# Small products of a scan split into two halves of heads, two GpSimd products taken a group earlier, and one integer step moved behind a mask, in a fused Mamba-2 scan and ELU feed-forward kernel

## The chip, the cores and the metric

The kernel runs on one core of one Trainium2 chip. The metric is the device time of one launch in microseconds (us). Before the change the median of three runs is 347.31 us (346.28 to 347.36). A profile is one more execution, recorded instruction by instruction.

The engines are named as in the profile: PE is the matrix engine TensorE, PEld its loading of weights, DVE is VectorE, ACT is ScalarE, POOL is GpSimd, and SP is the queue that issues nearly all transfers. L654 is line 654 of the kernel before the change.

## The reference: what is computed

A Mamba-2 scan in chunks, and then a feed-forward block with an ELU between its two products:

```python
# x (4, 8, 768, 32), a (4, 8, 768), B and C (4, 8, 768, 16); chunks of tokens per (batch, head)
cum = np.cumsum(log(a) of the chunk)
M = (C B^T) * exp(cum_i - cum_j) * causal
y = M x + (C state) * exp(cum)                     # inside the chunk + from the state before it
state = exp(sum of log a) * state + sum_j exp(cum_last - cum_j) B_j x_j^T
...
h = y_rows @ w_in            # (3072, 256) @ (256, 2048)
out = where(h > 0, h, exp(min(h, 0)) - 1) @ w_out   # @ (2048, 256)
```

All inputs are fp32. The result of the scan, with its heads side by side, is the input of the feed-forward block.

## The kernel before, in words

**Tiles of the scan.** A block `n` holds 256 tokens of one batch and all 8 heads; there are 12 blocks, and the scan works with chunks of 64 tokens, so a block has four, numbered by (u, v). Blocks 4 to 11 are handled in pairs (m, m+1). A pair needs, in this order: the decays L (a transfer from `flat`, a subtraction by `decay_sums`, L531 on POOL, an Exp on ACT, a mask on POOL); C scaled by exp(cum) (`turn_exp`, L459, here on POOL; its result is `cts`, the second half of the tile `bct`); `scores` (L577 on PE); `weigh` (L586 on DVE, gives M); `sums` (L607 on PE) and `states` (L622 and L624 on DVE, then a copy `Sx` masked by heads, L629 on POOL); `across` (L654 on PE: the part of y that comes from the state before a chunk); and `inside` (L672 on PE: M x, added to the same accumulators), after which y is shifted back to its place in `yT` (L689 on ACT, L687 on DVE).

**Small products.** `across` uses 32 rows by 64 columns of the array, at the position given by q (four pairs of heads, 32 rows each) and v. Its results go into four PSUM tiles y[t][v]: t is the half of the heads (q 0 and 1, or q 2 and 3). `inside` is called for one t at a time and has 64 rows by 32 columns. An fp32 product is two passes on PE, so that the profile counts two instructions for each product.

**Feed-forward.** For blocks 4 on, every fp32 product is put together from three products of shorter words. `l1_words` (L826) makes 128 columns of h for a pair of blocks: six passes of 128x512, into the PSUM tiles ps_w and ps_h. ACT reads ps_w into e (L834), DVE joins e and ps_h (L842), ACT takes Relu and Exp (L854, L855), DVE finishes the ELU (L861). A job then makes words of g for the second product: L916 on ACT, L917 on DVE (`g_low`), L893 on POOL (`g_words`). `second` is a generator: each step of it (here called a unit) is one slice of the second product, six passes of L975.

**Order.** Everything is written out by hand. For a pair of blocks n the loop over k = 0 to 15 issues one `l1_words`, `stage_scan(n, k)` for the scan of the next pair m, and some units of the second product for the pair before. At k = 9 come `scores`, at k = 10 `sums`, at k = 13 `across` and `inside`. This loop runs four times; the last has no scan left, so that `across` at k = 13 happens three times, for m = 6, 8 and 10. Pairs before that are handled elsewhere in the code (the pair (4, 5) calls `across` and `inside` without units between).

**PSUM.** There are eight banks. Seven are in the pool `p_a`, shared by all PE results, and one in `p_o`. A tile that takes a bank waits for the last reader of the tile that had it.

**Beginning.** The weights come as 64-bit floats. `w_sign` (L229), `w_high_a` (L237) and `w_high_b` (L244, a shift to the left) on DVE and `w_sum` (L254) on POOL make fp32 out of their words, piece by piece. `mask_heads(1)` (L476 on DVE) masks C of block 1 by heads for its `scores`.

The lines that the change touches are these:

```python
    def across(*ns, pool=p_a, tag="a"):
        y = [psum([P, len(ns), 2, Q], "ps_y") for _ in range(3)]
        y.append(pool.tile([P, len(ns), 2, Q], F32, tag=tag, name="ps_y"))
...
            if k == 13:
                y = across(m, m + 1, pool=p_o, tag="o")
                l2s(2)
                inside(y, m, m + 1, t=0)
                l2s(1)
                inside(y, m, m + 1, t=1)
```

Of the kernel before, what the change touches and what calls it, by code (L numbers as in the profile page):

```python
# [10 lines left out]
F32 = mybir.dt.float32  # L11
# [6 lines left out]
P = 128  # L18
# [15 lines left out]
def kernel(  # L34
# [56 lines left out]
    def psum(shape, name):  # L91
        return p_a.tile(shape, F32, tag="a", name=name)
# [129 lines left out]
    def w_sign(i, cols=slice(None), eng=nc.vector):  # L222
        w_parts_of(i)
        if eng is nc.gpsimd:
            eng.tensor_scalar(
                out=w_sgn[i][:, :, cols], in0=w_words(i)[1][:, :, cols].bitcast(mybir.dt.int32),
                scalar1=0.0, scalar2=2.0 ** 31, op0=ALU.is_lt, op1=ALU.mult)
            return
        nc.vector.tensor_scalar(  # L229
            out=w_sgn[i][:, :, cols], in0=w_words(i)[1][:, :, cols], scalar1=0x80000000,  # L230
            scalar2=None, op0=ALU.bitwise_and)
# [16 lines left out]
    def w_high(i):  # L248
        w_high_a(i)
        w_high_b(i)  # L250
# [222 lines left out]
    def mask_heads(n, eng=nc.vector):  # L473
        s = st[n]
        s["ctm"] = att.tile([P, 2, 2, P], F32, tag="ctm", name="ctm")
        eng.tensor_tensor(  # L476
            out=s["ctm"], in0=s["ct"].unsqueeze(2).to_broadcast([P, 2, 2, P]),
            in1=hmask2.unsqueeze(1).unsqueeze(3).to_broadcast([P, 2, 2, P]), op=ALU.mult)
# [158 lines left out]

        return 2 * D * v if n else 0

    def across(*ns, pool=p_a, tag="a"):  # L640


        y = [psum([P, len(ns), 2, Q], "ps_y") for _ in range(3)]
        y.append(pool.tile([P, len(ns), 2, Q], F32, tag=tag, name="ps_y"))
        y = [y[0:2], y[2:4]]
        for u in (1, 0):
            for at, n in enumerate(ns):
                for v in range(2):
                    Sx = starts.pop((n, u, v), None)
                    if Sx is None:  # L650
                        continue
                    for q in range(4):
                        rows, col = slice(32 * q, 32 * q + 32), (64 * q + shift(n, v)) % P
                        nc.tensor.matmul(  # L654
                            out=y[q // 2][v][col:col + 64, at, u],
                            lhsT=Sx[rows].rearrange("p k d -> p (k d)"),
                            rhs=st[n]["cts"][rows, u, Q * v:Q * v + Q],
                            start=(u == 1 and at == 0), stop=False,
                            tile_position=(32 * q, col), skip_group_check=True)
        return y  # L660

    def inside(y, *ns, t=None):

        for t in range(2) if t is None else (t,):
            for at, n in enumerate(ns):
                s = st[n]
                for u in range(2):
                    for v in range(2):
                        toks = slice(Q * v, Q * v + Q)
                        for q in range(4):  # L670
                            h, col = 4 * t + q, (D * q + shift(n, v)) % P
                            nc.tensor.matmul(  # L672
                                out=y[t][v][col:col + D, at, u],
                                lhsT=s["x"][toks, u, D * h:D * (h + 1)],
                                rhs=s["M"][h // 2][toks, u, h % 2], start=False, stop=True,
                                tile_position=(Q * v, col), skip_group_check=True)
            n = ns[0]
            if n // 2 not in yT:
                yT[n // 2] = ffn.tile([P, KC, 2, 2, P], F32, tag="yT", name="yT")
            out = yT[n // 2][:, t, n % 2:n % 2 + len(ns)]  # L680
            for v in range(2):
                k = shift(n, v)
                for at in (0, k) if k else (0,):
                    count, src = P - k, (at + k) % P
                    to, src = out[at:at + count, :, :, Q * v:Q * v + Q], y[t][v][src:src + count]
                    if t and (n == 1 or n > 4):
                        nc.vector.tensor_copy(to, src)  # L687
                    else:
                        nc.scalar.copy(out=to, in_=src)  # L689
        if t:  # L690
            for n in ns:
                st.pop(n)
# [414 lines left out]
    w_abs(3)  # L1107
    w_low(3, nc.scalar)
    w_sign(3)
    w_high(3)  # L1110
    mask_heads(1)
    turn_b(1)
    nc.scalar.activation(F[:, 1], F[:, 0], ACT.Exp)
    write_flat_exp()
# [209 lines left out]
    def stage_scan(n, k):  # L1324

        m = n + 2
        if k < 2:
            spread_exp(m + k)
        if k == 2:
            load_x(m)  # L1330
            load_x(m + 1)
        if 0 < k < 5 and (n > 4 or k > 1):
            turn_part(m + (k > 2), (k - 1) % 2)
        if k < 3:
            decay_exps(m + (k > 0), (k + 1) % 2)
        if k in (0, 1, 3, 4):
            decay_mask(m + (k > 1), (k + (k > 1)) % 2)
        if k in (5, 7):
            turn_part(m + k // 7, 2)
        if k in (6, 8):  # L1340
            scaled(m + k // 8, nc.gpsimd)
        if k == 10:
            turn_part(m, 3)
            turn_part(m + 1, 3)
        if k in (3, 5) and n > 4:
            load_b(m + (k > 3))
        if k in (6, 7) and m + 2 < NP:
            load_bc(m + k - 4)
        if k == 15 and m + 2 < NP:
            decay_exps(m + 2, 0)  # L1350

    for n in range(4, NP, 2):
        m = n + 2 if n + 2 < NP else None
        steps = second(n - 2)

        def l2s(count):
            for _ in range(count):
                next(steps)

        if n == 4:  # L1360
            l2s(1)
        if not m:
            scan_pools.close()
            late_pool = ctx.enter_context(tc.tile_pool(name="late", bufs=1))
        for k in range(16):
            if k < 13 and (n > 4 or k > 4):
                to_begin.append(lambda q=k + 3: job(n - 2, q))
            elif m and k > 12:
                to_begin.append(lambda q=k - 13: job(n, q))
            if not m and k in (4, 6, 8, 10, 12, 14, 15):  # L1370
                to_begin.append(lambda q=(4, 6, 8, 10, 12, 14, 15).index(k): late_job(q, late_pool))
            if k == 0 and n > 4:
                load_words(2)
            l1_words(
                n, k, m, [lambda q=q: weigh_two(m, q) for q in (2, 3) if m and k == 10],
                [lambda: states(m + 1)] if m and k == 11 else [])
            if k != 14 or not m:
                third_of_jobs()
            if n == 4 and k < 2:
                words_of_w(k + 2)  # L1380
            if n == 4 and 1 < k < 7:
                words_of_out(k + 1)
            if k in (2, 4, 6, 8, 10) and (k > 2 or n > 4):
                load_words(k // 2 + 2)
            if m and k == 14:
                nc.sync.dma_start(out=held, in_=yT[m // 2][Q:Q + 1, 0, 0, 0, Q:Q + 16])
            if m and k > 13:
                load_words(k - 14)
            if m:
                stage_scan(n, k)  # L1390
            begin_end()
            if n == 4 and k in (1, 2):
                low_of_w(k + 1)
                keep_words(k + 1)
            if n == 4 and 2 < k < 8:
                low_of_out(k)
            if not m:
                l2s(2)
                continue
            if k == 9:  # L1400
                l2s(1)
                scores(m, m + 1, pool=p_o, tag="o")
            l2s((2 - (n == 4 and k < 1), 2, 2, 2, 2, 2, 2, 2, 2, 1, 2, 2, 1, 0, 1, 0)[k])
            if k == 9:
                for q in range(2):
                    weigh_two(m, q)
            if k == 10:
                if m + 2 < NP:
                    for to in (m + 2, m + 3):
                        spread_cum(to)  # L1410
                sums(m, m + 1, pool=p_o, tag="o")
                states(m)
            if k == 13:
                y = across(m, m + 1, pool=p_o, tag="o")
                l2s(2)
                inside(y, m, m + 1, t=0)
                l2s(1)
                inside(y, m, m + 1, t=1)
            if k in (12, 13) and m + 2 < NP:
                decay_sums(m + k - 10)  # L1420
        if m:
            l2s(3)
        end_words()
        for _ in steps:
            pass
# [46 lines left out]
```

## Time and profile before

| | |
|---|---|
| runs | 346.28, 347.31, 347.36 us; median 347.31 |
| profiled execution | 345.99 us, of which the span of the profile is 344.1 us |
| granted clock of PE | 0.999 over the span |
| busy time in the span | PE 334.0, PEld 290.6, DVE 286.7, ACT 260.1, POOL 216.2 us |
| chain that ended last | PE 86%, DVE 5%, ACT 3%, POOL 2%, DMA 1%, issue 1% |
| `across` at k = 13, first start of L654 | 156.42, 208.06 and 260.55 us |
| the loop's first L826 of each pair that follows | 168.06, 220.50 and 272.4 us (about 52 us apart) |

The span runs from the first to the last instruction; the profiled execution is 1.9 us longer than its span. The chain that ended last is followed back from the end: at each step to what released the waiting instruction, or to the one before it on its engine. In a timeline row stand the start in us, the length in us from the first start to the last end of what is merged, the engine, the line, the operation, the tiles, the shape, the count of merged instructions, and in brackets the idle time of the engine before it with what ended it. Matmuls are pipelined: one pass of 128x256 lasts 0.28 us, but the next starts 0.12 us after it.

### The profile page before, as it was taken

Reading aid. Unit: us, or ns where it says so; the run is one execution under the profiler, and the core shown is the slowest. Engines: PE = TensorE matmul, PEld = TensorE weight load, DVE = VectorE, ACT = ScalarE, POOL = GpSimd, SP = SyncE. Lnnn points to the kernel's source line nnn. Section 1 sums busy time; section 2 is a strip of 40 time slices with the busy share of each in tenths; the row PEclk is TensorE's granted clock in tenths of the full one; section 3 lists DMA queues with packets and bytes.
Section 4 is the critical chain, followed back from the end, with each engine's and each line's share of the span. In section 5 each row is a group of like instructions: output and inputs, shape, how many; then the busy total and the mean of one; then the engine's idle time right before and its main releaser. Section 6 shows DMA issues by size and latency. Waiting matters only on the chain.

```text
span 344.1 us, 9650 instructions
## 1 busy us (share of the span) xinstructions
PE 334.0 (97%) x3742; PEld 290.6 (84%) x3742; DVE 286.7 (83%) x507; ACT 260.1 (76%) x537; POOL 216.2 (63%) x242
## 2 busy tenths in 40 slices
PE   8889999999999999999999998999998999999996
PEld 6568878888887888887899986898887899999995
DVE  2898998889797889896989987989995977997951
ACT  3887989699858699865898865798866688897601
POOL 5554545557989396989388968478965255775100
PEclk9999999999999999999999999999999999999999
DMA  8988979362578378660779390869340743240101
GB/s 145 244 221 192 316 132 257 71 153 76 187 143 314 128 208 273 201 175 10 270 193 231 105 284 20 272 192 187 105 168 2 277 137 146 79 161 0 33 0 61
DMA packets 82955, 54.79 MB, mean 159 GB/s; under 512 B 59038, under 2 KB 68574, under 8 KB 82910
## 3 DMA queue, kind: packets, MB, share of 16 engines
q1 hardware_dynamic: 80734, 53.98, 55.8%
q8 instruction: 29, 0.48, 0.6%
q10 hardware_dynamic: 2176, 0.20, 0.5%
q14 instruction: 16, 0.13, 0.1%
HBM read 44.53 MB, written 9.63 MB: 157 GB/s over the span
## 4 chain that ended last, share of the span: by engine, by line
PE 86%; DVE 5%; ACT 3%; POOL 2%; DMA 1%; issue 1%; DVEq 0%; POOLq 0%
PE ps_o L975 21%; PE ps_h L826 16%; PE ps_o L879 12%; PE ps_h L711 11%; PE ps_w L826 9%; PE ps_both L975 6%; PE ps_y L672 3%; PE ps_g L577 2%; PE ps_y L654 2%; DMA L<-flat 1%; DVE M L586 1%; PE ps_high L975 1%; DVE ps_h L842 1%; DVE g_low L917 1%; POOL bct L459 1%
## 5 line engine op out<-in xcount | busy, mean ns | idle before, releaser
L893 POOL TENSOR_TENSOR g_words<-g_words,g_low 128x512 fp32r<-128x512 f32 x62 | 82.4, 1332 | 55.6 <-DVE g_low L917 28.5
L975 PE MATMUL ps_o<-o_words,g_words 128*128 128x256 f32 x448 | 84.1, 285 | 0.0
L975 PEld LDWEIGHTS ps_o<-o_words,g_words 128*128 128x128 f32 x448 | 72.7, 190 | 6.2 <-POOL g_words L893 0.9
L854 ACT ACTIVATE e<-ps_h 128x512 f32<-128x512 f32 x72 | 43.1, 598 | 36.0 <-DVE ps_h L842 36.0
L861 DVE SCALAR_TENSOR_TENSOR g<-e,ps_h 128x512 f32<-128x512 f32 x72 | 49.3, 684 | 17.8 <-ACT e L855 15.8
L917 DVE SCALAR_TENSOR_TENSOR g_low<-g_words,g 128x512 fp32r<-128x512 f32 x72 | 63.4, 886 | 0.0
L975 PE MATMUL ps_o<-o_low,g_low 128*128 128x256 f32 x224 | 63.3, 283 | 0.0
L842 DVE SCALAR_TENSOR_TENSOR ps_h<-ps_h,e 128x512 f32<-128x512 f32 x72 | 49.8, 692 | 2.8 <-ACT e L834 2.8
L826 PE MATMUL ps_w<-y_both,w_words 128*128 128x512 f32 x144 | 48.7, 419 | 0.2 <-PE ps_h L826 0.2
L855 ACT ACTIVATE e<-e 128x512 f32<-128x512 f32 x72 | 45.5, 632 | 2.3
L834 ACT ACTIVATE e<-ps_w 128x512 f32<-128x512 f32 x72 | 42.0, 583 | 6.8 <-PE ps_w L826 6.8
L711 PE MATMUL ps_h<-yT,w_in 128*128 128x256 f32 (+1 forms) x208 | 45.1, 367 | 2.0 <-POOL w_in L254 1.1
L879 PE MATMUL ps_o<-w_out,g 128*128 128x256 f32 x192 | 45.5, 380 | 0.0
L826 PE MATMUL ps_h<-y,w_words 128*128 128x512 f32 x144 | 45.3, 395 | 0.0
L826 PE MATMUL ps_h<-y,w 128*128 128x512 f32 x144 | 44.7, 391 | 0.0
L916 ACT ACTIVATE g_words<-g 128x512 fp32r<-128x512 f32 x72 | 43.6, 624 | 0.0
L711 PEld LDWEIGHTS ps_h<-yT,w_in 128*128 128x128 f32 x208 | 36.4, 190 | 7.6 <-POOL w_in L254 1.6
L975 PEld LDWEIGHTS ps_o<-o_low,g_low 128*128 128x128 f32 x224 | 42.7, 191 | 0.0
L879 PEld LDWEIGHTS ps_o<-w_out,g 128*128 128x128 f32 x192 | 36.1, 190 | 5.5
L826 PEld LDWEIGHTS ps_h<-y,w 128*128 128x128 f32 x144 | 27.0, 188 | 6.3
L826 PEld LDWEIGHTS ps_h<-y,w_words 128*128 128x128 f32 x144 | 26.7, 188 | 6.6 <-PE ps_w L826 0.4
L826 PEld LDWEIGHTS ps_w<-y_both,w_words 128*128 128x128 f32 x144 | 23.5, 191 | 2.3 <-ACT e L854 0.6
(133 smaller groups left out, 555.7 us busy)
## 6 DMA issues: line engine op xcount, KB each, us to landing
w_words<-w_kept SPq DMA_DIRECT2D x28, 512.0 KB
w<-w_kept SPq DMA_DIRECT2D x28, 256.0 KB
L<-flat SPq DMA_DIRECT2D x20, 256.0 KB
w<-in_moe_w_out_dram SPq DMA_DIRECT2D x8, 512.0 KB
w_kept<-w_words SPq DMA_DIRECT2D x8, 512.0 KB
w<-in_moe_w_in_dram SPq DMA_DIRECT2D x7, 512.0 KB
xr<-in_x_dram SPq DMA_DIRECT2D x24, 128.0 KB
out_dram<-eo SPq DMA_DIRECT2D x18, 128.0 KB
```

What stands on the lines that cost most here:

```text
L711: nc.tensor.matmul(out=ps[:, j, toks], lhsT=w_in[i][:, k, j * P:(j + 1) * P], rhs=yT[n // 2][:, k, n % 2].rearrange("p u i -> p (u i)")[:, ...
L826: nc.tensor.matmul(out=ps, lhsT=lhs[:, k], rhs=rhs[:, k], start=k == 0 and lhs is not w0, stop=k == KC - 1 and lhs is not w1)
L834: nc.scalar.activation(e, both, ACT.Copy, scale=WORD)
L842: nc.vector.scalar_tensor_tensor(out=high, in0=high, scalar=WORD - 1.0, in1=e, op0=ALU.mult, op1=ALU.add)
L854: nc.scalar.activation(e, high, ACT.Relu, scale=-1.0)
L855: nc.scalar.activation(e, e, ACT.Exp, scale=-1.0)
L861: nc.vector.scalar_tensor_tensor(out=g_tile(n, m // 2)[:, m % 2].rearrange("p b i -> p (b i)"), in0=e, scalar=1.0, in1=h, op0=ALU.subtract ...
L879: nc.tensor.matmul(out=o_of[n][:, ts], lhsT=g_of[n // 2, j][:, m % 2, n % 2, ts * P:(ts + 1) * P], rhs=w_out[j][:, m % 2], start=(m == 0 a ...
L893: nc.gpsimd.tensor_tensor(out=out, in0=in0, in1=in1, op=ALU.subtract)
L916: yield nc.scalar.activation(words[:, 0], g, ACT.Copy, scale=NEAR / WORD)
L917: yield nc.vector.scalar_tensor_tensor(out=low, in0=words[:, 0].bitcast(F32), scalar=WORD, in1=g, op0=ALU.mult, op1=ALU.subtract)
L975: nc.tensor.matmul(out=ps, lhsT=lhs, rhs=rhs, start=lhs is both_g and first > 0 or lhs is g1 and first > 1, stop=last and lhs is not g1, s ...
```

## The change

`across` can now be called for one half of the heads. At k = 13 the first half is called with one PSUM tile from p_a and the one of `p_o`, then one unit, `inside` of that half, one unit, the second half with two tiles from p_a, one unit, and `inside` of the second half. The number of units is the same (three), the products and their number are the same. In `stage_scan` the two products of `turn_exp` come at k = 9 and no longer at k = 10; on POOL this puts both L459 ahead of one L893. At the beginning, `mask_heads(1)` comes ahead of both DVE steps of `w_high(3)` and no longer behind them. `starts.get` in the place of `starts.pop` lets both halves find Sx and issues nothing.

```diff
-    def across(*ns, pool=p_a, tag="a"):
-        y = [psum([P, len(ns), 2, Q], "ps_y") for _ in range(3)]
-        y.append(pool.tile([P, len(ns), 2, Q], F32, tag=tag, name="ps_y"))
-        y = [y[0:2], y[2:4]]
+    def across(*ns, pool=p_a, tag="a", halves=(0, 1)):
+        y = [None, None]
+        for t in halves:
+            y[t] = [psum([P, len(ns), 2, Q], "ps_y"), (p_a if t else pool).tile(
+                [P, len(ns), 2, Q], F32, tag="a" if t else tag, name="ps_y")]
...
-                    Sx = starts.pop((n, u, v), None)
+                    Sx = starts.get((n, u, v))
...
-                    for q in range(4):
+                    for q in range(2 * halves[0], 2 * halves[-1] + 2):
...
-    w_high(3)
     mask_heads(1)
+    w_high(3)
...
-        if k == 10:
+        if k == 9:
             turn_part(m, 3)
             turn_part(m + 1, 3)
...
-                y = across(m, m + 1, pool=p_o, tag="o")
-                l2s(2)
+                y = across(m, m + 1, pool=p_o, tag="o", halves=(0,))
+                l2s(1)
                 inside(y, m, m + 1, t=0)
+                l2s(1)
+                y = across(m, m + 1, halves=(1,))
                 l2s(1)
                 inside(y, m, m + 1, t=1)
```

More of the change, by code (lines that the diff above doesn't have):

```diff
@@ L1109 @@
     w_sign(3)
+    mask_heads(1)
     w_high(3)
-    mask_heads(1)
     turn_b(1)
```

## The prediction

> **What bounds the kernel now.** I read the page first: how busy each engine is, and which line the chain of work that ended last runs along. PE bounds the kernel, and there is little to win but its pauses and its own work.
>
> ```profile
> PE 334.0 (97%) x3742; PEld 290.6 (84%) x3742; DVE 286.7 (83%) x507; ACT 260.1 (76%) x537; POOL 216.2 (63%) x242
> ```
>
> Next the waits, of PE alone and stretch by stretch. From 30 us to the end PE itself waits in four places: 0.2 us at 92 to 110 us, and three times in `across` at k = 13, for ACT's L834 (0.8, 1.5 and 0.9 us):
>
> ```profile
> PE ps_y L654 <- ACT e L834: 3.2, 3, 1.5
> ```
>
> Third, the timeline of PE around the middle one, and the chain through the same place:
>
> ```profile
> 207.51 0.62 PE L826 MATMUL ps_h<-y,w 128*128 128x512 f32 x2
> 208.06 0.34 PE L654 MATMUL ps_y<-bct,Sx 32*64 32x64 f32 x8
> 209.88 0.84 PE L654 MATMUL ps_y<-bct,Sx 32*64 32x64 f32 x56 [1.47 <-ACT e L834]
> 210.65 0.51 PE L975 MATMUL ps_o<-o_words,g_words 128*128 128x256 f32 x2
> ```
>
> ```profile
> 207.99 0.60 ACT e L854
> 208.60 0.02 issue
> 208.62 0.63 ACT e L855
> 209.25 0.49 ACT e L834
> 209.74 0.14 issue
> 209.88 0.84 PE ps_y L654 x44
> ```
>
> The reader is to see that eight passes run and then PE stands still. The ninth belongs to v = 1; its bank is the one in which ps_w of the same k = 13 lies, and ACT reads that only after L854 and L855 of k = 12. The Sx are no hindrance (the last L629 ends at 207.15). So the pause is one of PSUM banks, of which `across` asks for four at once.
>
> **The split (L654).** I take the price of a small group as the time from where the next pass would have started to where it does start. Two passes of L826 take 0.46 (155.41 to 155.87), so without `across` the row at 207.51 would be followed at 207.97; L975 starts at 210.65: 2.68 us. Likewise 1.88 at 156 (155.87 + 0.46 = 156.33, L975 at 158.21) and 2.09 at 260 (260.46, 262.55). The three cost 6.65.
>
> A half has 32 passes (24 for m = 6, whose first chunk has no state) on four places of the array, where the whole has eight. The rows for both:
>
> ```profile
> 11.69 0.58 PE L654 MATMUL ps_y<-bct,Sx 32*64 32x64 f32 x24
> 12.20 0.88 PE L672 MATMUL ps_y<-M,xr 64*32 64x64 f32 x64
> ...
> 102.18 0.91 PE L654 MATMUL ps_y<-bct,Sx 32*64 32x64 f32 x64
> 103.02 1.51 PE L672 MATMUL ps_y<-M,xr 64*32 64x64 f32 x128
> ```
>
> The first, without shift, has four places: 24 passes take 0.51 from start to the next group's start. The second has eight: 64 take 0.84. The single starts lie in bursts, of four every 58 ns in the first and of eight every 59 ns in the second: a place takes one pass in 58 ns, whatever its neighbours do. So 24 passes of a half take 0.51, and 32 two bursts more, 0.51 + 8/4 x 0.058 = 0.63. Ahead of a small group lies 0.09 (L975 at 212.06, next due 212.18, L672 at 212.27). A half costs 0.72, or 0.60 with 24 passes. A first half at m = 6 and 8 has one more wait between its first four passes and the rest, as in the row of eight passes above (two bursts apart, then the rest): 0.1 each. Sum: 4 x 0.72 + 2 x 0.60 + 0.2 = 4.3. **The split gives 6.65 - 4.3 = 2.4 us.** Without pauses the whole would cost 0.93 (102.18 - 0.09 to 103.02), so three splits pay 4.3 - 2.8 = 1.5 for the 3.2 of waits and their startup.
>
> The new waits. By the banks that the program gets, the first half needs ps_w of k = 12 to be read (L834 ends at 206.05) and the `sums` in p_o to be used (the last L624 ends at 206.03); PE comes at 208.06. The second half needs ps_w of k = 13. PE comes there after first half, unit, `inside`, unit: 207.97 + 0.8 + 0.72 + 0.88 + 0.72 = 211.1 (a unit is 210.65 to 211.34, `inside` 212.18 to 213.06 with its edges), against 209.74 for ACT even if it gains nothing: 1.3 in hand, and about 1.7 at the other two. Behind a waiting PE would stand everything. Units: the second uses words that POOL ended at 208.40, the third has the same; covered by 2 us. At k = 14 and 15 the banks come from L689 of half 0 (1.15 us, now after about 210.4) and from L687 and L834: over 1 us in hand each.
>
> What is late next: the shifted copies of half 1 on DVE (L687), which stand idle 1.99 us for PE at 214.80 now, then DVE without a gap to 222 (L861, L842, L800, L810, L917), POOL's L893 to 221.87 and PE's first unit of the next pair at 221.92, for which PEld waits 0.3. This moves with PE, as DVE, ACT (idle 1.23 and 1.28) and POOL (idle 216.15 to 220.58) wait for it there. SP's loads stand behind the transfer `held`, which waits for L689; it comes earlier too, the first 768 KB are issued at 214.61 and used at 220.4, with the transfers' engines at 0.00 busy from 212 to 214.
>
> **L459 a group earlier.** No work is added, and no transfer is issued by it. On POOL both (1.43) pass one L893:
>
> ```profile
> 202.01 1.29 POOL L893 TENSOR_TENSOR g_words<-g_words,g_low 128x512 fp32r<-128x512 f32 x1 [2.85 <-ACT e L854]
> 203.26 1.43 POOL L459 TENSOR_TENSOR bct<-bct,ec 128x256 f32<-128x256 f32 x2
> ```
>
> POOL is idle for 2.85 ahead of that L893 (2.86 at 254, 1.60 at 150), so they fit there, the L893 is not later, and Sx and the L624 that wait for it (0.54) come up to 1.4 earlier. With the pause gone PE waits for none of that: **0**. Bounds: at 149.4 DVE's L917 (two operands in SBUF) falls beside them, 0.6 us later, with 1.3 in hand at PE; as a gain it can give the 0.3 that PEld waits for g_words, three times: -0.3 to 0.9.
>
> **The mask at the start.** DVE runs without a gap there, so the order alone saves nothing on it; `scores` may start when PE is free (20.54 + 8 x 0.216 = 22.27) and not at 22.60.
>
> ```profile
> 21.77 0.68 DVE L476 TENSOR_TENSOR ctm<-bct,hmask 128x512 f32<-128x512 f32 x1
> 22.56 1.31 DVE L459 TENSOR_TENSOR bct<-bct,ec 128x256 f32<-128x256 f32 x1
> 23.79 0.67 DVE L732 SCALAR_TENSOR_TENSOR g<-e,ps_h 128x512 f32<-128x512 f32 x1
> ```
>
> Those 0.3 go into the next wait (L711 at 24.61, 0.90 for L732), unless L732 is earlier. It could be: L459 has two operands in SBUF and ends at 23.87, right after POOL's L254 (21.99 to 23.58) which ran beside it; half of L800's 0.68 would be its own time. L254 will start some 0.6 later (its input L244 is now last), so L459 may run ahead of it. Then w_in is ready at about 24.2 and L711 starts 0.35 earlier; the waits up to 28.87 (Sx, 0.3) let the gain grow to 0.65. From below: L254 is 0.68 later with 1.00 in hand, and POOL's L343 and ACT's L1134 behind it are 0.6 later, with 1.98 of idle ACT ahead; -0.3. I take **0.2**, nearer to nothing, since PE comes just as a bank is released at 44.91 and 51.53 (0.05 in hand), where 0.3 can be lost again.
>
> The Trainium skill says on this ("SBUF - State Buffer", section "Who interferes with whom") that a VectorE instruction with two SBUF inputs and a GpSimd one that reads SBUF exclude each other, and that whichever starts first holds the port to its end. The trace agrees (L917 at 210.49 takes 2.32 beside L531, where others take 0.69). By this rule the upper end, 0.65, would be the sum's third term, and the total 3.1.
>
> **Sum:** 2.4 + 0 + 0.2 = 2.6. The profiled execution, 345.99, would be 343.4. The median of the runs shown is 347.31, 1.3 above it; I take the same difference from that: **344.7**.
>
> **Rivals.**
> 1. *Two at a time.* Passes of a half share their rows in pairs (q fixed, v = 0 and 1), and all q of a half write to two banks. If only two run side by side, 32 passes take 16 x 0.058 + 0.15 = 1.08, a half costs 1.17 (0.94 for 24): 4 x 1.17 + 2 x 0.94 = 6.56, no gain, about 347.2. For it: no group with just these four places is in the trace. Against: the eight of 102.18 have the same pairs and the same two row groups for each bank. The Trainium skill ("TensorEngine Tiling (Array Packing)", "Restrictions and Gotchas", Gotcha 1) says that different row tiles cannot access one PSUM bank at the same time; by that rule this rival would hold, but the bursts of eight at 102.18 disagree. Chance 0.06.
> 2. *The wait moves on.* PE is earlier, but the first units of the next pairs wait for L893 as now, because DVE's run behind the copies does not move (L531 on POOL, 1.94, blocking its L800 and L810). All or most of the 2.4 is lost there: 346.3 to 347.3. For it: 0.05 in hand at 169.49, 221.92 and 273.82. Against: idle DVE, ACT and POOL just ahead of it. Chance 0.12.
> 3. *Slower: one at a time.* If the passes of a half run one by one, a half takes 32 x 0.058 = 1.86 more or less and costs 2.1 (1.6 for 24): 4 x 2.1 + 2 x 1.6 = 11.6 against 6.65, 5.0 slower, 352. It turns to a loss when a half costs over 1.11 (6.65 / 6). For and against it speaks what does for rival 1, and the burst of four at 11.69 besides. Chance 0.07.
> 4. *More from the start or from L459.* 0.4 to 1.3 on top of the forecast, about 343.8. Chance 0.15; within it the range is cut at 343.5.
>
> Forecast 0.60, 344.2 to 345.9. The remainder of each case's spread is that of the runs, 1.1 between lowest and highest. Faster by over 0.3% (below 346.27; a smaller difference can't be told from none here): forecast, rival 4 and 0.02 of rival 2: 0.77. Within 0.3%: rival 1 and 0.08 of rival 2, 0.14. Slower: rival 3 and 0.02 of rival 2, 0.09. The range, 343.5 to 347.2, leaves out rival 3 and parts of 1 and 4.
>
> **What the profile after would show.** Right: no L654 row with a wait for L834 over 0.2; six L654 groups of 24 or 32, each 0.6 to 0.8 from its due start to the next group; L826 of k = 14 some 1.3 us closer to L826 of k = 13 at 208; L459 ahead of a waiting L893; L476 ended before 21.6 with L577 at about 22.3. Wrong: a half over 1.1, or PE waiting for L893 at the first L975 of a pair by more than the 0.3 of now.

## The result, and the profile after

| | before | after |
|---|---|---|
| median | 346.33 us (345.72 to 347.36, 6 runs) | 342.88 us (341.77 to 343.15, 6 runs) |
| ratio | | 0.9888, 95% interval 0.9864 to 0.9912 |
| profiled execution | 345.99 us, span 344.1 | 343.07 us, span 341.3 |

The change makes the kernel faster by 3.1 to 4.7 us by that interval. Run again with experiments 5 to 8, it had 342.53 us and a ratio of 0.9911 (0.9884 to 0.9937). The forecast was 344.7 with a range from 343.5, so the direction held and the time lies 0.6 below the range, 1.8 below the forecast. One thing is needed to read the medians: in 12 of 42 later runs of the kernel before, the granted clock was 0.993 or 0.994 and not 0.998 to 1.000, and their median is 347.28, against 345.86 for the other 30.

The first rows are the busy times and the chain of the page of the kernel after. PE now makes up 92% of the chain, where it had 86%:

```profile
PE 335.0 (98%) x3742; PEld 291.4 (85%) x3742; DVE 285.4 (84%) x507; ACT 259.3 (76%) x537; POOL 215.3 (63%) x242
...
PE 92%; SPq 4%; DVE 1%; DMA 1%; POOL 0%; issue 0%; DVEq 0%; POOLq 0%
```

The waits of PE (total us, times, longest) have no row of `across` left; L654 is L655 now, and every line behind it has one more (in e8 and e9, whose edit adds a line, one more again):

```profile
PE ps_h L712 <- POOL w_in L254: 1.9, 3, 0.8
PE ps_idle L278 <- DVE idle L264: 1.1, 1, 1.1
```

The timeline of PE at the middle group, in place of the pause of 1.47:

```profile
206.47 0.62 PE L827 MATMUL ps_h<-y,w 128*128 128x512 f32 x2
207.01 0.69 PE L655 MATMUL ps_y<-bct,Sx 32*64 32x64 f32 x32
207.64 0.50 PE L976 MATMUL ps_o<-o_words,g_words 128*128 128x256 f32 x2
207.98 0.28 PE L976 MATMUL ps_o<-o_low,g_low 128*128 128x256 f32 x1
208.10 0.40 PE L976 MATMUL ps_o<-o_words,g_words 128*128 128x256 f32 x2
...
208.54 0.86 PE L673 MATMUL ps_y<-M,xr 64*32 64x64 f32 x64
...
210.24 0.69 PE L655 MATMUL ps_y<-bct,Sx 32*64 32x64 f32 x32
210.86 0.50 PE L976 MATMUL ps_o<-o_words,g_words 128*128 128x256 f32 x2
...
212.65 0.72 PE L827 MATMUL ps_w<-y_both,w_words 128*128 128x512 f32 x2
```

A half takes 0.63 from its start to the next group's. Behind it the first two passes of a unit take 0.50, where the next two take 0.40: leaving a small group costs 0.10, which the prediction left out. The row of ACT that frees the bank of the second half:

```profile
207.57 0.58 ACT L835 ACTIVATE e<-ps_w 128x512 f32<-128x512 f32 x1
```

The measure for all that follows is the stretch of a group: from the start of the last L827 pass of k = 13 (L826 before the change) to the first of k = 14. It holds the three units, `across` and `inside`, whatever their order. Before, the three stretches are 6.22, 7.01 and 6.42, together 19.65 us; after, 5.86, 5.96 and 5.86, together 17.68: 1.97 less.

At the beginning, the rows of POOL and PE before (those of DVE stand in the prediction):

```profile
21.99 1.59 POOL L254 TENSOR_TENSOR w_in<-mag,w_in 128x512 uint32<-128x512 uint32 x1 [1.15 <-ACT e L724]
24.61 1.97 PE L711 MATMUL ps_h<-yT,w_in 128*128 128x256 f32 x8 [0.90 <-DVE g L732]
```

And the rows of DVE, POOL and PE after:

```profile
20.56 1.10 DVE L476 TENSOR_TENSOR ctm<-bct,hmask 128x512 f32<-128x512 f32 x1
...
22.65 0.42 DVE L459 TENSOR_TENSOR bct<-bct,ec 128x256 f32<-128x256 f32 x1
23.30 0.69 DVE L733 SCALAR_TENSOR_TENSOR g<-e,ps_h 128x512 f32<-128x512 f32 x1 [0.23 <-ACT e L732]
```

```profile
22.87 1.32 POOL L254 TENSOR_TENSOR w_in<-mag,w_in 128x512 uint32<-128x512 uint32 x1 [1.75 <-DVE mag L244]
```

```profile
22.33 0.69 PE L577 MATMUL ps_g<-ctm,bct 32*64 32x128 f32 x32
24.25 1.99 PE L712 MATMUL ps_h<-yT,w_in 128*128 128x256 f32 x8 [0.79 <-POOL w_in L254]
```

L459 starts 0.22 before L254 and takes 0.42, where it took 1.31. From the first DVE instruction of this part (L476 at 20.56; before, L237 at 20.28) to the last start of L712 (28.39; before 28.87) it is 7.83, and was 8.59: 0.76 less. This stretch is called the beginning below. What lies ahead of it is left out because it differs between executions: in the kernel before, ACT's L205 at 15.43 hardly waits; in the kernel after, it waits 1.19 us for a transfer of weights and starts at 16.51.

### The profile page after: what moved, and what is told of

Read it like the earlier page. It is cut to its first block, busy times and chain, and to the rows that moved or that the text cites. A ratio compares the mean times of both kernels' runs of the same rounds, so it can differ in the third digit from the quotient of the medians.

```text
span 341.3 us, 9645 instructions
## 1 busy us (share of the span) xinstructions
PE 335.0 (98%) x3742; PEld 291.4 (85%) x3742; DVE 285.4 (84%) x507; ACT 259.3 (76%) x537; POOL 215.3 (63%) x242
## 4 chain that ended last, share of the span: by engine, by line
PE 92%; SPq 4%; DVE 1%; DMA 1%; POOL 0%; issue 0%; DVEq 0%; POOLq 0%
PE ps_o L976 24%; PE ps_h L827 19%; PE ps_o L880 12%; PE ps_h L712 11%; PE ps_w L827 10%; PE ps_both L976 6%; PE ps_y L673 3%; SPq L184 2%; PE ps_y L655 2%; PE ps_g L577 2%; PE ps_st L607 1%; PE ps_high L976 1%; DMA xr<-in_x_dram 1%; SPq L140 1%; SPq L156 0%; POOL w_in L254 0%
## 5 line engine op out<-in xcount | busy, mean ns | idle before, releaser
L894 POOL TENSOR_TENSOR g_words<-g_words,g_low 128x512 fp32r<-128x512 f32 x62 | 82.4, 1333 | 52.4 <-DVE g_low L918 29.0
L835 ACT ACTIVATE e<-ps_w 128x512 f32<-128x512 f32 x72 | 41.9, 582 | 9.2 <-PE ps_w L827 9.2
L827 PE MATMUL ps_w<-y_both,w_words 128*128 128x512 f32 x144 | 48.6, 419 | 0.0
L712 PE MATMUL ps_h<-yT,w_in 128*128 128x256 f32 (+1 forms) x208 | 45.1, 367 | 1.9 <-POOL w_in L254 1.9
L827 PE MATMUL ps_h<-y,w_words 128*128 128x512 f32 x144 | 45.4, 396 | 0.0
L827 PE MATMUL ps_h<-y,w 128*128 128x512 f32 x144 | 44.6, 391 | 0.0
L917 ACT ACTIVATE g_words<-g 128x512 fp32r<-128x512 f32 x72 | 43.6, 624 | 0.0
L712 PEld LDWEIGHTS ps_h<-yT,w_in 128*128 128x128 f32 x208 | 36.3, 190 | 7.6 <-POOL w_in L254 2.8
L827 PEld LDWEIGHTS ps_h<-y,w 128*128 128x128 f32 x144 | 27.0, 188 | 6.3
L827 PEld LDWEIGHTS ps_h<-y,w_words 128*128 128x128 f32 x144 | 26.6, 188 | 6.6 <-issue 0.8
L827 PEld LDWEIGHTS ps_w<-y_both,w_words 128*128 128x128 f32 x144 | 23.6, 191 | 1.8
```

The costliest lines, as they stand in the source:

```text
L712: nc.tensor.matmul(out=ps[:, j, toks], lhsT=w_in[i][:, k, j * P:(j + 1) * P], rhs=yT[n // 2][:, k, n % 2].rearrange("p u i -> p (u i)")[:, ...
L827: nc.tensor.matmul(out=ps, lhsT=lhs[:, k], rhs=rhs[:, k], start=k == 0 and lhs is not w0, stop=k == KC - 1 and lhs is not w1)
L835: nc.scalar.activation(e, both, ACT.Copy, scale=WORD)
L894: nc.gpsimd.tensor_tensor(out=out, in0=in0, in1=in1, op=ALU.subtract)
L917: yield nc.scalar.activation(words[:, 0], g, ACT.Copy, scale=NEAR / WORD)
```

## Experiments

Each heading marked "same chip" holds kernels that ran on one chip and share the runs of the kernel before.

### 1 to 4, same chip: each part alone, and the whole across behind three units

Kernel before: 346.11 us (20 runs). **e1_mask**: the kernel before with the mask moved.

```diff
-    w_high(3)
     mask_heads(1)
+    w_high(3)
```

> The kernel before with the third edit alone: the mask of heads ahead of both DVE steps of the fourth piece. Theory (a port between DVE and GpSimd is what the order decides): L459 takes about 0.42 us and not 1.31, L254 starts about 0.6 later, PE waits at about 24.3 for L254 and no longer for L732; 0.4 to 0.9 us less than before. Rival (DVE's order alone, no port): L459 stays at about 1.3 and the time is within 0.3 of before.

345.11 us, ratio 0.9957 (0.994 to 0.9974): 1.0 less by the medians, just over the theory's 0.9. L459 takes 0.42 and the beginning 7.82, 0.77 less than before; the three groups take 19.82, so they gain nothing. The theory of the port holds, and DVE's order alone does not explain it (the rival had L459 at 1.3).

**e2_early**: the kernel before with both L459 at k = 9.

```diff
-        if k == 10:
+        if k == 9:
             turn_part(m, 3)
             turn_part(m + 1, 3)
```

> The kernel before with the second edit alone: both L459 a group sooner. Theory (the bank of ps_w is what across waits for, and the exponent products only delay ACT's reading of it): DVE, and ACT's L834 of k = 13, come 0.4 to 0.6 earlier in each pair, the three pauses of L654 shrink from 3.2 us to 1.5 to 2.2 in total; 0.8 to 1.6 us less than before. Rival (Sx, made by GpSimd behind L459, is what across waits for): the pauses go altogether, 3 us less. Second rival (the prediction's term): no gain, within 0.3 of before.

344.86 us, ratio 0.9954 (0.9936 to 0.9972). Its waits of PE:

```profile
PE ps_y L654 <- ACT e L834: 2.6, 3, 1.3
```

The time is within the theory's 0.8 to 1.6 less, but the pauses shrink from 3.2 to 2.6 and not to 2.2. They do not go, as they would if `across` waited for Sx. The groups take 19.07, 0.58 less: 0.5 more in the first, 0.5 less in each of the others. The 0.5 more is what the prediction's bound named: DVE's L917 at 148.99 takes 1.17 beside L459, where before it took 0.68. The interval says at least 0.97. This execution is 1.15 shorter in its span than the profiled one before, and the other half of that lies where the edit does not reach: 0.23 by 30 us and 0.33 at 109.45.

**e3_split**: the kernel before with `across` in halves, and nothing else (the new `across` itself is as in the change and is left out here).

```diff
-                y = across(m, m + 1, pool=p_o, tag="o")
-                l2s(2)
+                y = across(m, m + 1, pool=p_o, tag="o", halves=(0,))
+                l2s(1)
                 inside(y, m, m + 1, t=0)
+                l2s(1)
+                y = across(m, m + 1, halves=(1,))
                 l2s(1)
                 inside(y, m, m + 1, t=1)
```

> The kernel before with the first edit alone: across in two halves with units between. Theory: each half costs 0.72 us on PE, no pause is left, 2.3 us less than before, and the second and third edit add 0.5 to 1 from the start and nothing in the loop. Rival (the second half's bank is still late without the earlier exponent products): L654 waits in the second halves, 1 to 1.8 us less than before.

343.97 us, ratio 0.9926 (0.9904 to 0.9949). No wait of `across`; each group takes 5.86, together 17.58, which is 2.07 less than before. The second half never waits.

**e4_three_ahead**: the changed kernel with `across` whole again, behind all three units, and both `inside` behind it.

```diff
-                y = across(m, m + 1, pool=p_o, tag="o", halves=(0,))
-                l2s(1)
+                l2s(3)
+                y = across(m, m + 1, pool=p_o, tag="o")
                 inside(y, m, m + 1, t=0)
-                l2s(1)
-                y = across(m, m + 1, halves=(1,))
-                l2s(1)
                 inside(y, m, m + 1, t=1)
```

> The changed kernel with across whole again, behind all three units of k = 13, and both inside right after it. Theory (units give ACT the time to free the bank, the split itself only costs): no pause, a whole across costs 0.93 us where two halves cost 1.44, 0.5 to 0.9 less in each pair, 1.5 to 2.5 us less than the changed kernel, 5 to 6 less than before. Rival (the next waits: g_words of the units, or the banks of the l1 of k = 14, which ACT and DVE free only after inside): the changed kernel's time or up to 2 us more than it.

341.79 us, ratio 0.9864 (0.9836 to 0.9891): 1.1 below the changed kernel's median and 0.7 below its median on the chip of experiments 5 to 8, less than expected. The groups take 4.67, 6.70 and 4.75. The timeline of the middle one shows a pause of another kind, "issue", within `inside`:

```profile
208.54 1.36 PE L673 MATMUL ps_y<-M,xr 64*32 64x64 f32 x113
...
211.65 0.34 PE L673 MATMUL ps_y<-M,xr 64*32 64x64 f32 x15 [1.75 <-issue]
...
211.92 0.74 PE L827 MATMUL ps_w<-y_both,w_words 128*128 128x512 f32 x2
```

In this stretch the table of DMA queues (packets, MB, share) has one packet of a queue named instruction, from 209.06 to 210.37, and the page has 29 of them:

```profile
q8 instruction: 1, 0.02, 1.0%
```

```profile
q8 instruction: 29, 0.48, 0.6%
```

0.48 MB in 29 packets are 16.5 kB each; PE has 3742 loads and 3742 products, 7484 instructions and some 100 for events, 29.6 times 256. Counted from 0 at the first one of the trace, the late product is instruction 5313. The only pause of PE outside `across` from 30 us on in the kernel before (the row that the prediction gave as 0.2 at 92 to 110 us) stands at 3009, nine times 256 earlier. From one start to the next it takes 0.63 there, where 0.23 is usual:

```profile
109.45 0.70 PE L826 MATMUL ps_w<-y_both,w_words 128*128 128x512 f32 x2 [0.24 <-PE ps_h L826]
```

So a new theory: PE's instructions come in blocks of 256, and where PE reaches a border before the block is there, it stands still.

### 5 to 8, same chip: how many units ahead, and where the borders lie

Kernel before: 345.33 us (11 runs). **e5_after_again** is the changed kernel.

> The changed kernel itself once more, beside the three variants that follow. Both theories: 342.9 us again (342.4 to 343.4), 3.3 to 3.9 less than before, and no wait of PE for L835 in across.

342.53 us, ratio 0.9911 (0.9884 to 0.9937): 2.8 less by the medians, a little under what was expected. The groups take 5.86 each.

**e6_two_ahead** and **e7_one_ahead**: the whole `across` behind two units and behind one.

```diff
-                y = across(m, m + 1, pool=p_o, tag="o", halves=(0,))
-                l2s(1)
+                l2s(2)
+                y = across(m, m + 1, pool=p_o, tag="o")
                 inside(y, m, m + 1, t=0)
                 l2s(1)
-                y = across(m, m + 1, halves=(1,))
-                l2s(1)
                 inside(y, m, m + 1, t=1)
```

```diff
-                y = across(m, m + 1, pool=p_o, tag="o", halves=(0,))
+                l2s(1)
+                y = across(m, m + 1, pool=p_o, tag="o")
                 l2s(1)
                 inside(y, m, m + 1, t=0)
-                l2s(1)
-                y = across(m, m + 1, halves=(1,))
                 l2s(1)
                 inside(y, m, m + 1, t=1)
```

> Change 2 and 3 kept; two units, then the whole across, inside of half 0, one unit, inside of half 1. Theory (PSUM bank, read by ACT at about 208.15): PE comes to the whole at 208.3 and doesn't wait, a whole costs 0.93, so each group takes about 0.7 less than the two halves of the changed kernel (2 x 0.72 + one edge of 0.1 against 0.93): 2.1 less. Theory on the pause that PE made in the last inside of the middle group of the kernel with three units ahead (its block of 256 instructions came late): the pause comes back at the same instruction but smaller, 0.8 to 1.2 and not 1.8, because the unit between gives the fetch 0.7 more time. Together 341.3 to 342.2, 0.8 to 1.4 less than the changed kernel. Rival 1 (that pause was an accident of one execution): none here, 340.5 to 341.0. Rival 2 (the pauses of across are not a bank's): a wait of over 0.3 for L835 in across in spite of two units ahead, and the changed kernel's time or more.

341.79 us, ratio 0.9882 (0.9859 to 0.9905). The time is as expected. No wait of `across`; the pause is at the same product, instruction 5313, and smaller, 0.65 where 0.8 to 1.2 was expected:

```profile
210.00 0.72 PE L673 MATMUL ps_y<-M,xr 64*32 64x64 f32 x49
211.37 0.34 PE L673 MATMUL ps_y<-M,xr 64*32 64x64 f32 x15 [0.65 <-issue]
```

> Change 2 and 3 kept; one unit, then the whole across, one unit, inside of half 0, one unit, inside of half 1. Theory (bank, read by ACT at a time that does not hang on PE): each unit put ahead takes 0.72 off the pause, so the middle group's 1.3 (whole without a unit ahead, L459 early) is 0.4 to 0.7 here and the other two have at most 0.2; the three groups cost 3.4 to 3.9 in place of 4.3, so 342.2 to 342.8, 0.3 to 0.9 less than the changed kernel. Rival (the pause follows PE: ACT is behind PE by a fixed time, or the wait is for Sx): the pauses stay at 1.3 and 0.6 to 0.8, and the time is 0.7 to 1.5 above the changed kernel's, 343.6 to 344.4.

341.50 us, ratio 0.9875 (0.9851 to 0.9899), better than expected. The pause that is left (0.5) is in the first group; the middle one has 0.13. Without a unit ahead these two have 1.17 and 0.83 (experiment 11): one unit takes off 0.7 in both, as the theory of the bank has it, and the rival, a pause that follows PE, is refuted. Each run of e6 and e7 is below each run of e5 (at most 342.11 against at least 342.25); between e6 and e7 the runs do not decide.

**e8_three_ahead_shift**: e4 with 60 instructions less at PE's beginning; these products keep PE busy and compute nothing that is read.

```diff
-    small_idle_products(29)
-    idle_product(3)
+    small_idle_products(13)
+    idle_product(4)
+    idle_product(1)
```

> The kernel with three units ahead of the whole across, and both insides back to back, with 60 instructions less at PE's beginning (16 small products without use fewer, two wide ones in their place, about equally long). The computation is untouched. Theory (the pause of 1.8 in the middle group is the fetch of a block of 256 instructions that PE reaches 1.7 us after the block before): the border moves 60 instructions on, behind the last inside and into wider products, and the pause is gone or below 0.3: 339.8 to 340.6, 1.3 to 1.9 less than the 341.8 of the unshifted kernel. Rival (a transfer, or something else at that place in the program or in that one execution): 341.4 to 342.2, with the pause at the same product as before or without one.

342.17 us, ratio 0.9889 (0.9862 to 0.9917). The middle group is free of the pause (4.75), but the first has it now, at instruction 4033, and `inside` at 12.73 has 1.0, at 449:

```profile
157.69 1.41 PE L674 MATMUL ps_y<-M,xr 64*32 64x64 f32 x118
160.93 0.33 PE L674 MATMUL ps_y<-M,xr 64*32 64x64 f32 x10 [1.84 <-issue]
```

The expected time was missed, since only the middle group had been thought of, and 342.17 lies within the rival's 341.4 to 342.2. The places decide for the theory all the same: 449, 3009, 4033 and 5313 leave 193 when divided by 256, and the pause went where the border went. (Why 193 and not 0, the trace does not show.)

### 9 to 12, same chip: a better shift, the port, and each part left out

Kernel before: 345.94 us (11 runs). **e9_three_ahead_shift96**: e4 with 96 instructions less.

```diff
-    small_idle_products(29)
+    small_idle_products(4)
+    idle_product(4)
     idle_product(3)
```

> The kernel with three units ahead of the whole across, with 96 instructions less at PE's beginning (25 small products without use fewer, two wide passes more, about equally long). Theory (PE pauses at the border of a block of 256 instructions when it comes there less than about 3.5 us after the border before): with this shift one border lies about 100 to 175 instructions inside each dense group and the next some 50 or more products behind it; by the times of the unshifted kernel that leaves at most 0.2 us of pause in the first group and 0.2 in the third, in place of 1.8 in the second and of 1.8 in the first with a shift of 60. So 339.9 to 340.7, about 1.3 less than the unshifted kernel's 341.8, and no pause of over 0.4 in inside. Rival (the pauses are no matter of blocks): a pause of over 1 in one of the groups again, and 341.4 to 342.4.

340.81 us (340.29 to 341.51), ratio 0.9843 (0.9824 to 0.9863), the lowest of all and 0.1 above the expected range. The groups take 4.67, 4.75 and 4.75; the middle one:

```profile
208.27 0.91 PE L656 MATMUL ps_y<-bct,Sx 32*64 32x64 f32 x64
209.11 1.51 PE L674 MATMUL ps_y<-M,xr 64*32 64x64 f32 x128
210.55 0.73 PE L828 MATMUL ps_w<-y_both,w_words 128*128 128x512 f32 x2
```

One pause of 0.54 is left, in an earlier `inside` at 103.25, at instruction 2753 (193 again); the expectation had none over 0.4. Its 3.5 us between two borders are no rule: in e4 PE passed border 4033 (at 158.53) 1.57 us after border 3777 without a pause. The block's packet had landed early there, at 156.86.

**e10_exp_after_pad**: the changed kernel with two memsets on DVE ahead of the first L459.

```diff
     rest_of_sums()
+    pad = const.tile([P, P], F32, name="pad")
+    nc.vector.memset(pad, 0.0)
+    nc.vector.memset(pad, 0.0)
     turn_exp(1)
```

> The changed kernel with two small memsets (0.17 each, of a tile that nothing reads) on DVE just ahead of the first L459, at 22.6 us. The computation is untouched. Theory (the port: L459 is short, 0.42, only because it starts 0.2 before L254 on POOL, and is held to L254's end when it starts after it): L459 starts at about 22.95, after L254, and takes 1.2 to 1.5; L733 behind it comes 1.0 to 1.3 later, and the stretch from the eight L712 ahead of scores to the last L712 of the beginning grows from 7.93 to 8.6 to 9.2; 0.7 to 1.2 slower than the changed kernel, 343.2 to 344.0. Rival (what counts is only that the mask is earlier, and that scores don't wait for it): L459 stays at 0.4 to 0.7, the stretch grows by at most 0.3, and the time is within 0.4 of the changed kernel's.

343.37 us, ratio 0.9924 (0.99 to 0.9948), as expected; experiment 12 with the short L459 has 342.92 on the same chip. The two intervals overlap, so it is the profile that decides. The rows of DVE, POOL and PE:

```profile
22.20 0.17 DVE L1129 MEMSET pad<- 128x128 f32 x1
22.28 1.38 DVE L459 TENSOR_TENSOR bct<-bct,ec 128x256 f32<-128x256 f32 x1
```

```profile
22.11 1.27 POOL L254 TENSOR_TENSOR w_in<-mag,w_in 128x512 uint32<-128x512 uint32 x1 [1.75 <-DVE pad L1128]
```

```profile
24.41 1.97 PE L712 MATMUL ps_h<-yT,w_in 128*128 128x256 f32 x8 [1.71 <-DVE g L733]
```

L459 starts 0.17 after L254 and ends 0.28 after it: 1.38 and not 0.42. PE waits 1.71 where it waited 0.8, and the beginning takes 8.86 and not 7.8. 0.35 us of memsets cost 1.0; the mask is as early as in the changed kernel, so its place alone is not what pays. L476, too, is longer after the change: there it starts 0.26 after POOL's L423 (20.30, 0.82 long), and takes 1.10 us, where it took 0.68.

**e11_no_split**: changes 2 and 3 without the split, the order of the kernel before at k = 13.

```diff
-                y = across(m, m + 1, pool=p_o, tag="o", halves=(0,))
-                l2s(1)
+                y = across(m, m + 1, pool=p_o, tag="o")
+                l2s(2)
                 inside(y, m, m + 1, t=0)
-                l2s(1)
-                y = across(m, m + 1, halves=(1,))
                 l2s(1)
                 inside(y, m, m + 1, t=1)
```

> Changes 2 and 3 without the split: across whole, two units, inside of half 0, one unit, inside of half 1. Theory (bank): the pauses are those of the kernel with change 2 alone, 2.6 in all (0.4 to 1.3 each), not 3.2; so the split is worth 4.3 against 6.0 here, and not against 6.65: 1.5 to 2.0 on top of the other two, 344.0 to 344.7 where the changed kernel has 342.5 to 342.9. Rival (the terms add up as if alone): 2.1 to 2.4 above the changed kernel.

343.43 us, ratio 0.9921 (0.99 to 0.9942), lower than expected. Its waits:

```profile
PE ps_y L655 <- ACT e L835: 2.3, 3, 1.2
```

The groups take 18.70: the split is worth 1.1 on top of the other two, where it is worth 2.07 alone. The terms share the pause, even more than the theory had said.

**e12_split_mask**: changes 1 and 3, L459 in the loop at k = 10.

```diff
-        if k == 9:
+        if k == 10:
             turn_part(m, 3)
             turn_part(m + 1, 3)
```

> Changes 1 and 3, L459 in the loop a group later as before. Theory (change 2 pays only where across waits for a bank that ACT holds up): on top of the split it is worth nothing, 342.4 to 343.2, within 0.4 of the changed kernel. Rival (it pays by itself, as alone, by Sx or by POOL's words coming sooner): 0.8 to 1.3 above the changed kernel, 343.4 to 344.2.

342.92 us, ratio 0.9894 (0.9874 to 0.9914); the groups take 17.58, as with change 2. On top of the split, L459 a group earlier is worth nothing.

## Why the prediction was right in direction, and missed the time

**The base failed.** The step was: "The median of the runs shown is 347.31, 1.3 above it; I take the same difference from that". Those were three runs; with the three more of the result the median is 346.33, and later medians of the same kernel are 346.11 (20 runs), 345.33 and 345.94 (11 each). So 0.98 of the 1.82 between 344.7 and 342.88 is this term, put at 1.3 above the profiled execution where 346.33 is 0.34 above it. The other 0.84 is that the medians differ by 3.45 and not by 2.6; on the chip of experiments 5 to 8 they differ by 2.80. Against its own execution the forecast was 343.4, and the profiled execution of the kernel after has 343.07.

**The split: mechanism right, 2.4 forecast, 2.07 measured** (19.65 to 17.58 in e3). A half with 32 passes is 0.63 and 0.09 as forecast. With 24 it is 0.63 too and not 0.51: the single starts show four bursts of four passes and then four bursts of two, since the places of the chunk without a state stay empty, so there are eight bursts in both. The 0.1 put on two of the first halves did not come. By luck these two misses cancel (6 x 0.72 = 4.3, as forecast). Left out was 0.10 behind each small group: six halves cost 6 x (0.63 + 0.09 + 0.10) = 4.92, the three wholes 6.65 + 3 x 0.10 = 6.95, and the difference is 2.03. The 0.1 more in the changed kernel's first profile (5.96 in the middle group) is a pass of `inside` at 212.37 that comes late, at the same instruction 5313.

**No new wait: right.** ACT has read ps_w of k = 13 at 208.15 (L835 starts at 207.57 and takes 0.58), and PE comes to the second half at 210.24: 2.1 in hand, where 1.3 was forecast.

**L459 a group earlier: right, 0.** Alone it gives 0.58 in the groups (e2), without the split but beside the mask 1.1 (19.82 in e1, 18.70 in e11), on top of the split nothing (e12): it pays only where `across` waits for ACT.

**The mask: mis-sized, 0.2 forecast, 0.7 measured.** Old order 8.48 to 8.59 (before, e2, e3), new order 7.80 to 7.83 (nine profiles; 7.51 in e8). The second step that failed is the choice of the value, "nearer to nothing, since PE comes just as a bank is released at 44.91 and 51.53": what had been won at 29.5 us (0.48 by the starts of PE's products) was nearly all there at 60 us (0.40). The cause named was the right one. The Trainium skill ("SBUF - State Buffer", "Who interferes with whom") says that the one that starts first holds the port to its end; by that rule the forecast gave 0.65, and e10, which turns the order of two starts round by 0.35 us of memsets, agrees with it: 1.38 against 0.42.

**The sum.** 2.07 + 0 + 0.7 = 2.8 where 2.6 was forecast: two sizes missed in opposite directions, so that the nearness of the sum is luck. The spans of the two profiled executions differ by 2.80: 1.97 in the groups, 0.48 by 30 us (0.76 less the 0.28 by which this part of DVE began later) and 0.40 at 109.45, where the kernel before had a pause that neither profile of the changed kernel has, less 0.05 elsewhere. The 0.40 is an accident of the execution.

**The rivals.** Two at a time and one at a time are refuted by a half of 0.63 (they had 1.08 and 1.86 for the passes). The Trainium skill's Gotcha 1 ("TensorEngine Tiling (Array Packing)", "Restrictions and Gotchas"), by which two row tiles can't use one bank together, would have given the first of them; no run here shows it. The wait that moves on is refuted by the list of waits, which has no L894. (In e4 PE does wait for it, 0.3 at 166.69: it is what comes next.) The fourth, more from the start, is what happened, 0.5 of it.

**What stays open:** why the medians of the first comparison differ by 3.45, where the groups and the beginning give 2.8; why e2's interval begins at 0.97, where the groups give 0.58; and how long a block of instructions takes from its request. Only its landing is visible: PE went on 1.3 to 1.6 after it (107.83 to 109.42 before, 210.37 to 211.65 in e4, 159.50 to 160.93 in e8).

## What to carry to other kernels

Add what a step saves to several executions' median, not to three runs that happen to be high; and when two edits attack one pause, price the second on what the first has left. Where a unit of other work can go ahead of a group that waits for four banks, that beats splitting the group (e6 and e7 against e5): the split pays the way into and out of a small group twice and fills four places where the whole fills eight (here 1.64 for two halves, 1.03 for a whole that does not wait), the order pays nothing. Before a VectorE product of two SBUF tiles is moved beside a GpSimd one, look which of them starts first by tenths of a microsecond: here the loser was prolonged past the other's end (1.31 and 1.38 where 0.42 was its own time).

## What the runs showed that was not expected

PE's instruction stream is a resource with a place. Dense groups of small products use 256 instructions in about 1.5 us (128 passes of `inside`, with their loads, in 1.44), and a border inside such a group costs up to 1.84 us. The same program with 60 or 96 instructions less at its beginning has the pause in another place or hardly at all: the three groups take 16.12 in e4, 16.23 in e8 and 14.17 in e9. The times say it less clearly: the medians of 341.79, 342.17 and 340.81 are from three chips, and the intervals of their ratios touch or overlap. The traces decide. With a border at each instruction that leaves 193, and the 29 packets taken in order, none of the 392 borders in the fourteen traces is passed sooner than 1.2 us after its packet has landed, and each pause of over 0.3 at a border ends 1.2 to 1.6 after the landing. The Trainium skill ("Runtime: NRT & Kernel Launch", "Instruction fetch mechanics") says that the stream is refilled in blocks of 16 KiB, 256 instructions, by the sequencer's own DMA queue, and that this is mostly hidden. The trace agrees with the blocks (29 packets, 0.48 MB) and with hidden for wide products; not for groups as dense as these. And the same border can be late in one execution and not in another: at instruction 3009 the kernel before, e3 and e6 lost 0.4 each (0.63, 0.66 and 0.59 between two starts where 0.23 is usual), while the two profiles of the changed kernel lost nothing. In these three the packet began to move 3.7 to 3.9 us after PE had passed the border before; in the other unshifted kernels it was at most 3.4 us.
